# A transformer block's forward and backward on one core: the turn between the two passes rearranged

## The chip, the cores and the metric

The kernel runs on one core of a Trainium2 chip. The metric is device time in microseconds (us) of one execution; lower is better. Engines are named as in the profile: PE (TensorE, matrix products), PEld (its weight loads), DVE (VectorE), ACT (ScalarE), POOL (GpSimd), SP (SyncE). SP and POOL issue nearly all DMAs here, each from an in-order queue.

## The reference

One token (`x` of 640 values) goes through attention over a cache of 8192 keys with 32 heads of 192, and then through an MLP; both are wrapped in a conditioned layer norm. The outputs are the result and the gradients by `x`, the K and V caches, `wq`, `wo`, `w3`, `w4`, `c` and `w_mod`.

```python
mod = (silu(c) @ w_mod).reshape(1, 6, 1, -1)        # sa, ca, ga, sb, cb, gb
h = layernorm(x) * (1 + ca) + sa
q = h @ wq                                          # 32 heads of 192
p = softmax(q k^T * 192 ** -0.5); o = p v           # per head, 8192 keys
x = x + ga * (o @ wo)
h = layernorm(x) * (1 + cb) + sb
x = x + gb * B(h)
# B with S = 1: the shifted mixing term is zero, so
# B(h) = h + gelu(layernorm(h) @ w3) @ w4           # 640 -> 1536 -> 640
# outputs: x, and the vector-Jacobian product with grad_out for
# x, k_cache, v_cache, wq, wo, w3, w4, c, w_mod
```

K and V are 100.7 MB each, and so are dK and dV. K and V are read in the forward pass, V once more in the backward pass, and dK and dV are written there.

## The kernel before, in words

**Tiles.** Keys lie as 128 partitions by 64 (`J`). A head's K, V, dK or dV is two halves, each a tile of 128 x 32 x 192 in bf16 (1536 KB). K halves, and later dV and dK halves, rotate through five tiles of the pool `big`. V halves go through three tiles (`fv`), and in the backward pass through three more (`bv`), which are laid over the memory of the forward products (`fprod`) and of the scaled keys (`fek`).

**Forward loop** (`for i in range(1, HQ + 2)`). Head `i` gets its scores: DVE multiplies K with the broadcast q (`fwd_mult`, recorded under the helper's line L131, tile `prod`), PE sums over the 192 with an identity matrix (`fwd_ssum`, L355), DVE reduces (`fwd_red`, L359), PE and DVE find the maximum, ACT takes the exponential (`fwd_exp`, L376) with its row sum. Meanwhile head `i - 1` is worked off in four quarters: ACT and DVE scale K's rows by E into `EK` (`fwd_scale_act`, L390; `fwd_scale_dve`, L398), with E itself as a further column, and PE multiplies V with EK (`fwd_kvA`, L415; `fwd_kvB`, L423; `fwd_kvK`, L431). These products give o, and V^T E K, which is kept per head in `MA_all` and `MB_all`: with it the backward pass has dq without reading K again. `fwd_ao` (L475) adds each pair of heads' o @ wo to `ao_c`. The loop's last two passes only work off the last head (31).

**The turn.** W3 and W4 are loaded on POOL's queue into three `big` tiles in the last passes. `dg_some` (L496) takes products of W4 with the incoming gradient on DVE. `w3T_some` (L622) transposes W3 on PE, with ACT copies, in 15 groups of four blocks, some inside the gaps (`fill`) of the layer norms' short chains (`ln_cols`, `ln_bwd_cols`). Then come the two layer norms, W3's product u (L727), gelu and its derivative, dn2 by the transposed W3 (L755), the two layer norms' backward, and do of the last pair of heads by the transposed Wo (L1065). `ring_load` reads V halves and batches of Wo ahead on SP, in a ring of six slots.

**Backward loop** (`for i in range(HQ)`, heads 31 down to 0). DVE multiplies V with do in place (`bwd_mult`, tile `V_sb`), PE sums it (dP, L886). dV is the outer product of p and do, 20 rows of a half on ACT (L894) and 12 on DVE (L871), stored by POOL (L900). `bwd_ds` gives dS, and `bwd_dk` the outer product of dS and q, stored by POOL (L915). `hook` works off Wo's batches (`bwd_ttr`) and dq by `MA_all` and `MB_all` (`fin_dq_mm`, `fin_dq`). Further jobs for dWq, dWo, dW3, dW4 and dw_mod are hung into fixed passes.

The order on PE, DVE and ACT is the written one: `pin_order` ties each instruction to the one before it on its engine. DMA queues are in written order too, each DMA waiting for its tile.

Of the kernel before, what the change touches and what calls it, by code (L numbers as in the profile page):

```python
# [20 lines left out]
def kernel(  # L21
# [97 lines left out]
    nc.vector.memset(eps_c, LN_EPS)  # L119
    mask_lo = const.tile([P, 1], FP32, name="mask_lo")  # L120
# [31 lines left out]
    def ln_cols(x_c, pfx, fill=lambda k: None):  # L152
# [11 lines left out]
        nc.scalar.activation(out=std, in_=v_ps, func=ACT.Sqrt, bias=eps_c[:, 0:1], scale=1.0)  # L164
        rstd = ccol(1, pfx + "_rstd")
        nc.vector.reciprocal(out=rstd, in_=std)
        fill(1)
# [54 lines left out]
    big = ctx.enter_context(tc.tile_pool(name="big", bufs=5))  # L222

    def big_tile(name):
        return big.tile([P, JH, DH], BF16, name=name, tag="big")
# [61 lines left out]
    q_ps = kb_ps[:, 512 - NQC : 512]  # L287
# [32 lines left out]
    def load_v(pool, h, t):  # L320
        tl = pool.tile([P, JH, DH], BF16, name="V_sb")
        nc.sync.dma_start(out=tl, in_=V_hd[h][:, t * JH : (t + 1) * JH, :])
        return tl

    def load_fwd(h, t, kind):
        if not 0 <= h < HQ:
            return
        if kind == "v":
            st[h]["V"].append(load_v(fv, h, t))
        elif (h, t) not in K_st:  # L330
            K_st[h, t] = load_k(h, t)
# [40 lines left out]
    def fwd_exp(h, st):  # L372
        negm = fsm.tile([P, 1], FP32, name="negm")
        nc.vector.tensor_reduce(out=negm, in_=st["sm"][:, P : 2 * P], axis=AX.X, op=ALU.max, negate=True)  # L374
        E_f = fsm.tile([P, J], FP32, name="E_f")
        nc.scalar.activation(out=E_f, in_=st["sm"][:, 0:J], func=ACT.Exp, bias=negm, scale=1.0, accum_out=rowsum[:, h : h + 1])  # L376
        st["E_f"], st["EK"] = E_f, []

# [6 lines left out]
    def fwd_scale_act(h, q, st):  # L385
        t, r = divmod(q, 2)
        EK = fek.tile([P, JQ, DE], BF16, name="EK")
        for jj in range(NA):
            j = q * JQ + jj
            nc.scalar.activation(out=EK[:, jj, 0:DH], in_=K_st[h, t][:, r * JQ + jj, :], func=ACT.Copy, scale=st["E_f"][:, j : j + 1])  # L390
        st["EK"].append(EK)

# [15 lines left out]
    def fwd_kvA(h, q, st):  # L408
        (a0, a1), _, _, _, _ = head_split(h)
        if q == 0:  # L410
            st["A_ps"], st["B_ps"] = bank("a"), bank("b")
        t, r = divmod(q, 2)
        V_sb, EK = st["V"][t], st["EK"][q]
        for jj in range(JQ):
            nc.tensor.matmul(st["A_ps"][:, 0 : DH + 1], lhsT=V_sb[:, r * JQ + jj, a0:a1], rhs=EK[:, jj, 0 : DH + 1], start=(q == 0 and jj == 0), stop=(q == 3 and jj == JQ - 1))  # L415

    def fwd_kvB(h, q, st):
        _, (b0, b1), _, _, _ = head_split(h)
        t, r = divmod(q, 2)
        V_sb, EK = st["V"][t], st["EK"][q]  # L420
        for jj in range(JQ):
            g = 64 * (jj % 2)
            nc.tensor.matmul(st["B_ps"][g : g + 64, 0 : DH + 1], lhsT=V_sb[:, r * JQ + jj, b0:b1], rhs=EK[:, jj, 0 : DH + 1], start=(q == 0 and jj < 2), stop=(q == 3 and jj >= JQ - 2))  # L423

    def fwd_kvK(h, q, st, last=False):
        if h == HQ - 1 and not last:
            return
        EK = st["EK"][q]
        for jj in range(0, JQ, 2):
            g = 32 * (jj // 2 % 4)  # L430
            nc.tensor.matmul(kb_ps[g : g + 32, 0 : 2 * DH], lhsT=hot_bf[:, HQ - 1 - h : 2 * HQ - 1 - h], rhs=EK[:, jj : jj + 2, 0:DH], start=(h == 0 and q == 0 and jj < 8), stop=(h == HQ - 1 and q == 3 and jj >= JQ - 8), skip_group_check=True)  # L431
# [12 lines left out]
    def fwd_keep(h, st):  # L444
        (a0, a1), (b0, b1), bp, ca_, cb_ = head_split(h)
        op = 64 - bp
        nc.scalar.copy(out=MA_all[:, h, :], in_=st["A_ps"][:, 0 : DH + 1])
        Bt = fsm.tile([P, DH + 1], FP32, name="Bt")
        nc.scalar.copy(out=Bt[bp : bp + 64, :], in_=st["B_ps"][op : op + 64, 0 : DH + 1])
        st["Bt"] = Bt  # L450

    def fwd_keepB(h, st):
        (a0, a1), (b0, b1), bp, ca_, cb_ = head_split(h)
        Bt = st["Bt"]
        add(MB_all[bp : bp + 64, h // 2, :], st["B_ps"][bp : bp + 64, 0 : DH + 1], Bt[bp : bp + 64, :])
# [15 lines left out]
    def fwd_ao(hp, wo, sm):  # L471
        c0 = 3 * hp
        for r in range(NDC):
            for cc in range(3):
                nc.tensor.matmul(sm[:, 408 + r : 409 + r], lhsT=wo[:, cc, r * P : (r + 1) * P], rhs=o_col_bf[:, c0 + cc : c0 + cc + 1], start=(cc == 0), stop=(cc == 2))  # L475

    def fwd_ao_add(hp, sm):
        if hp == 0:
            dve_copy(ao_c, sm[:, 408 : 408 + NDC])
        else:  # L480
            add(ao_c, ao_c, sm[:, 408 : 408 + NDC])
# [4 lines left out]
    def w3n(i, lo, hi):  # L486
        return w_t[0][:, i * F + lo : i * F + hi] if i < 4 else w_t[1][:, lo:hi]

    def w4n(f, lo, hi):
        return w_t[1][:, F + f * D + lo : F + f * D + hi] if f < 7 else w_t[2][:, (f - 7) * D + lo : (f - 7) * D + hi]  # L490

    def dg_some(f0, f1):
        jk_t = fpr.tile([P, JH, DH], BF16, name="prod").rearrange("p j d -> p (j d)")
        for f in range(f0, f1):
            jk = jk_t[:, f % 4 * D : (f % 4 + 1) * D]
# [6 lines left out]
    warm = ccol(1, "warm")  # L502
# [18 lines left out]
    fv = ctx.enter_context(tc.tile_pool(name="fv", bufs=3, side="right", reuse_waits="tile"))  # L521
# [5 lines left out]
    fek_cm = tc.tile_pool(name="fek", bufs=4, reuse_waits="tile")  # L527
# [4 lines left out]
    for i in range(1, HQ + 2):  # L532
        if i == HQ + 1:
            nc.scalar.activation(out=warm, in_=eps_c, func=ACT.Sqrt)
# [4 lines left out]
        if pp:  # L539
            fwd_kv(i - 2, 3, st[i - 2])  # L540
# [7 lines left out]
        if i == HQ - 1:  # L548
            w_t = [flat(big_tile(f"w_t{k}")) for k in range(2)]
            nc.gpsimd.dma_start(out=w_t[0].rearrange("p (i n) -> p i n", n=F), in_=B_w3[0 : 4 * P, :].rearrange("(i p) n -> p i n", p=P))  # L550
            nc.gpsimd.dma_start(out=w_t[1][:, 0:F], in_=B_w3[4 * P : 5 * P, :])
            nc.gpsimd.dma_start(out=w_t[1][:, F : F + 7 * D].rearrange("p (f n) -> p f n", n=D), in_=B_w4[0 : 7 * P, :].rearrange("(f p) n -> p f n", p=P))
        if i == HQ:
            w_t.append(flat(big_tile("w_t2")))
            nc.gpsimd.dma_start(out=w_t[2][:, 0 : 5 * D].rearrange("p (f n) -> p f n", n=D), in_=B_w4[7 * P : 12 * P, :].rearrange("(f p) n -> p f n", p=P))
# [41 lines left out]
        load_fwd(i + 2, 0, "k")  # L597
        if n:
            fwd_mult(i + 1, 0, st[i + 1])
        if c:  # L600
            fwd_pairs(i, st[i])
        if i == HQ:
            dg_some(0, 7)
    dg_some(7, NFC)
    SB = [1024]
    w_t.append(flat(big_tile("w_t3")))
    NB3 = JH * DH // P

    def w3T(blk, n=1):
        if blk < NB3:  # L610
            return w_t[3][:, blk * P : (blk + n) * P]
# [3 lines left out]
    w3T_next = [0]  # L615

    def w3T_some(n):
        for g in range(w3T_next[0], min(w3T_next[0] + n, NFC * NDC // 4)):
            t_ps = bank("s", 2, "t_ps", SB[0])
            for k in range(4):  # L620
                f, i = divmod(4 * g + k, NDC)
                nc.tensor.matmul(t_ps[:, k * P : (k + 1) * P], lhsT=w3n(i, f * P, (f + 1) * P), rhs=ident_bf, start=True, stop=True)  # L622
            nc.scalar.copy(out=w3T(4 * g, 4), in_=t_ps[:, 0:512])
        w3T_next[0] += n

# [11 lines left out]
    w3T_some(3)  # L637
    fwd_kvK(HQ - 1, 0, st[HQ - 1], True)
    fwd_kvK(HQ - 1, 1, st[HQ - 1], True)
    sm = bank_c("sm_ps")  # L640
    fwd_ao(HH - 1, st[HQ - 1]["wo"], sm)
    fwd_ao_add(HH - 1, sm)
    fwd_kvK(HQ - 1, 2, st[HQ - 1], True)
    kb_sb = const.tile([P, 2 * DH], FP32, name="kb_sb")
# [3 lines left out]
    psum_cm.__exit__(None, None, None)  # L648
# [499 lines left out]
```

## Time and profile before

| | |
|---|---|
| median of 3 runs | 1395.56 us (1395.42 to 1396.38) |
| profiled execution | 1394.78 us, span 1393.0 us |
| PE busy | 864.9 us (62%) |
| DVE busy | 1072.7 us (77%) |
| ACT busy | 962.8 us (69%) |
| DMA moved | 570.81 MB, mean 410 GB/s; SP's queue 339.16 MB, POOL's 229.85 MB |
| mean granted PE clock | 0.78 |

The profile is of one execution; its own time is 0.78 us below the median. Busy shares are averages over stages with different limits: the forward pass is the first 550 us, the turn some 40 us, the backward pass the rest. Windows and timelines count from the span's start. "Idle before <-X" in a timeline is how long the engine had been idle ahead of an instruction, and what ended that.

### The profile page before, as it was taken

To read this page: it belongs to the slowest core of one execution; us is meant where nothing else is said; L and a number is where in the kernel's file an instruction comes from. 1 tells how busy PE (TensorE), PEld (TensorE's weight loads), DVE (VectorE), ACT (ScalarE), POOL (GpSimd) and SP (SyncE) were. 2 spreads that over 40 slices of the span, in tenths; PEclk is the share of its full clock that TensorE was granted. 3 is DMA by queue.
4 is the path that set the end of the run, shared out by engine and by line. 5 is a ranking of instruction groups with operands and counts; after the bars stand their busy time and mean duration, and the time that the engine had idled before them with its cause. 6 is when DMAs were issued, how large, how long until landed. Compare 5 with 4: busy or idle time off the path is not lost. (4 is left out here: it accounts for less than half of the span.)

```text
span 1393.0 us, 28144 instructions
## 1 busy us (share of the span) xinstructions
PE 864.9 (62%) x11519; PEld 676.1 (49%) x11519; DVE 1072.7 (77%) x1276; ACT 962.8 (69%) x2633; POOL 115.2 (8%) x207
## 2 busy tenths in 40 slices
PE   3799999999999999747636652444332444322442
PEld 3577777777777777535525541223221233212331
DVE  3588788887788877699978974975767659667796
ACT  1387778787788777686885586567666766556582
POOL 0000000000000000011101110211111111111011
PEclk9799999999999999566656666666776666765666
DMA  9999999999999999699999999999999999999988
GB/s 393 414 417 420 419 419 421 418 417 417 410 415 420 406 421 353 234 376 398 426 426 426 426 428 426 428 427 427 429 426 424 424 425 422 421 419 415 412 375 369
DMA packets 71711, 570.81 MB, mean 410 GB/s; under 512 B 6878, under 2 KB 18398, under 8 KB 31134
## 3 DMA queue, kind: packets, MB, share of 16 engines
q1 hardware_dynamic: 46496, 339.16, 59.2%
q0 software_dynamic: 25056, 229.85, 39.2%
q8 instruction: 90, 1.47, 0.4%
q14 instruction: 39, 0.32, 0.1%
q10 hardware_dynamic: 30, 0.00, 0.0%
HBM read 343.08 MB, written 225.91 MB: 408 GB/s over the span
## 5 line engine op out<-in xcount | busy, mean ns | idle before, releaser
L894 ACT ACTIVATE dV<-do_pb,PF 128x192 bf16<-128x192 bf16 x1260 | 439.5, 440 | 87.6 <-DMA out_dram<-dK 59.6
L886 PE MATMUL dP_ps<-V_sb,ident_bf 128*128 128x256 bf16 x1536 | 235.3, 329 | 256.1 <-DVE V_sb L131 256.0
L390 ACT ACTIVATE EK<-K_sb,E_f 128x192 bf16<-128x192 bf16 x1024 | 362.4, 442 | 4.0 <-PE kb_ps L294 2.6
L886 PEld LDWEIGHTS <-ident_bf 128*128 128x128 bf16 x1536 | 180.9, 118 | 310.9 <-issue 179.4
L871 DVE TENSOR_TENSOR dK<-dS,q_pb 128x6144 bf16<-128x6144 bf16 (+1 forms) x67 | 213.0, 3211 | 42.6 <-DMA out_dram<-dK 39.0
L131 DVE TENSOR_TENSOR prod<-K_sb,q_pb 128x6144 bf16<-128x6144 bf16 x64 | 214.3, 3349 | 5.4 <-DMA K_sb<-in_A_k_cache_dram 5.4
L131 DVE TENSOR_TENSOR V_sb<-V_sb,do_pb 128x6144 bf16<-128x6144 bf16 x64 | 211.8, 3351 | 6.9 <-DMA V_sb<-in_A_v_cache_dram 6.9
L415 PE MATMUL ps_a<-EK,V_sb 128*128 128x193 bf16 x2048 | 199.9, 250 | 2.8 <-DMA V_sb<-in_A_v_cache_dram 2.2
L415 PEld LDWEIGHTS <-V_sb 128*128 128x128 bf16 x2048 | 171.8, 99 | 21.5 <-issue 13.9
L871 DVE TENSOR_TENSOR dV<-P2h,do_pb 128x2304 bf16<-128x2304 bf16 (+1 forms) x65 | 87.3, 1369 | 57.6 <-DMA out_dram<-dV 50.4
L398 DVE TENSOR_TENSOR EK<-K_sb,P2h 128x1536 bf16<-128x1536 bf16 x128 | 121.3, 948 | 0.0
L423 PE MATMUL ps_b<-EK,V_sb 128*64 128x193 bf16 x2048 | 112.4, 252 | 0.0
L355 PE MATMUL S_ps<-prod,ident_bf 64*64 64x256 bf16 x3072 | 101.9, 281 | 13.4 <-DVE prod L131 13.4
L355 PEld LDWEIGHTS <-ident_bf 64*64 64x64 bf16 x3072 | 86.9, 111 | 33.5 <-issue 29.2
L423 PEld LDWEIGHTS <-V_sb 128*64 128x64 bf16 x2048 | 84.3, 110 | 20.2 <-issue 16.6
L376 ACT ACTIVATE E_f<-sm_ps,negm 128x64 f32<-128x64 f32 x32 | 10.1, 315 | 108.2 <-DVE negm L374 108.2
L359 DVE TENSOR_REDUCE S<-S_ps 128x128 f32<-128x1024 f32 x32 | 39.2, 1225 | 47.5 <-PE S_ps L355 47.5
L900 POOL DMA_DIRECT2D out_dram<-dV x65 | 34.9, 536 | 461.7 <-ACT dV L894 288.0
L431 PE MATMUL kb_ps<-EK,hot_bf 128*32 128x384 bf16 x1024 | 66.2, 337 | 0.0
L972 PEld LDWEIGHTS <-ident_bf 128*128 128x128 bf16 x112 | 13.9, 124 | 86.7 <-issue 83.1
L194 ACT CAST do_pb<-bc_ps 128x384 bf16<-128x384 f32 x16 | 7.5, 470 | 69.1 <-PE bc_ps L190 69.1
L930 ACT ACTIVATE wq_o<-wq_bc,ha_f 128x1536 bf16<-128x1536 bf16 x12 | 18.5, 1566 | 47.6 <-DMA out_dram<-wq_o 47.6
(249 smaller groups left out, 820.0 us busy)
## 6 DMA issues: line engine op xcount, KB each, us to landing
V_sb<-in_A_v_cache_dram SPq DMA_DIRECT2D x126, 1536.0 KB, 13.7
K_sb<-in_A_k_cache_dram SPq DMA_DIRECT2D x64, 1536.0 KB, 14.4
out_dram<-dV POOLq DMA_DIRECT2D x63, 1536.0 KB, 19.4
out_dram<-dK POOLq DMA_DIRECT2D x63, 1536.0 KB, 20.6
wq<-in_A_wq_dram SPq DMA_DIRECT2D x3, 2560.0 KB, 34.0
wo_t<-in_A_wo_dram SPq DMA_DIRECT2D x16, 480.0 KB, 14.4
out_dram<-dwo POOLq DMA_DIRECT2D x16, 480.0 KB, 19.5
wq<-in_A_wq_dram SPq DMA_DIRECT2D x4, 1920.0 KB, 29.4
```

The costliest lines, as they stand in the source:

```text
L131: nc.vector.tensor_tensor(out=out, in0=a, in1=b, op=ALU.mult)
L355: nc.tensor.matmul(st["S_ps"][c0 : c0 + 64, r, t * JH : (t + 1) * JH, :], lhsT=ident_bf[64 * r : 64 * r + 64, 64 * r : 64 * r + 64], rhs=p ...
L359: nc.vector.reduce_sum(out=st["S2"], in_=st["S_ps"], axis=AX.X)
L390: nc.scalar.activation(out=EK[:, jj, 0:DH], in_=K_st[h, t][:, r * JQ + jj, :], func=ACT.Copy, scale=st["E_f"][:, j : j + 1])
L398: nc.vector.tensor_tensor(out=EK[:, NA:JQ, 0:DH].rearrange("p j (d r) -> p j d r", r=2), in0=K_st[h, t][:, r * JQ + NA : (r + 1) * JQ, :]. ...
L415: nc.tensor.matmul(st["A_ps"][:, 0 : DH + 1], lhsT=V_sb[:, r * JQ + jj, a0:a1], rhs=EK[:, jj, 0 : DH + 1], start=(q == 0 and jj == 0), sto ...
L423: nc.tensor.matmul(st["B_ps"][g : g + 64, 0 : DH + 1], lhsT=V_sb[:, r * JQ + jj, b0:b1], rhs=EK[:, jj, 0 : DH + 1], start=(q == 0 and jj < ...
L431: nc.tensor.matmul(kb_ps[g : g + 32, 0 : 2 * DH], lhsT=hot_bf[:, HQ - 1 - h : 2 * HQ - 1 - h], rhs=EK[:, jj : jj + 2, 0:DH], start=(h == 0 ...
L871: nc.vector.tensor_tensor(out=o.rearrange("p j (d r) -> p j d r", r=2), in0=pairs[:, :, None, :].to_broadcast([P, n, NP2, 2]), in1=vec.rea ...
L886: nc.tensor.matmul(bst[h]["dP_ps"][:, t * JH : (t + 1) * JH, :], lhsT=ident_bf, rhs=V_sb[:, :, k * DS : (k + 1) * DS], start=(k == 0), sto ...
L894: nc.scalar.activation(out=o[:, jj, :], in_=doh, func=ACT.Copy, scale=bst[h]["PF"][:, j0 + jj : j0 + jj + 1])
L900: st2.dma_start(out=dV_hd[h][:, j0 + r0 : j0 + r1, :], in_=o[:, r0:r1, :])
```

## The change

The last head (31) gets no scaled keys and no products V^T E K. Its o comes from 128 products with single columns of E (`sum_rows`, `fwd_o_mm`), its exponentials are written in bf16 straight into `E_all`, and its dq comes in the backward pass from its unscaled K, which stays in two `big` tiles until then (`dq_last`). The forward loop ends one head earlier. W3 and W4 are loaded on SP's queue, behind K and V of the last heads. The second V half of head 30 stays in its tile and isn't read again. `fprod`'s and `fek`'s memory becomes free earlier, so that V halves are read ahead sooner; the first Wo batch goes into a `big` tile instead of a ring slot. The transposes of W3, the d_g products and h2 are cut in pieces and put in other gaps. u, dn2, h2, do and the last dq use spare columns of the PSUM bank of `kb_ps`. Head 31's dV is made by DVE alone, its first half stored in three pieces; the first dV half of head 30 is moved ahead of the loop. The order of the `big` tiles is written out by hand.

```diff
...
-        E_f = fsm.tile([P, J], FP32, name="E_f")
+        E_f = E_all[:, h, :] if h == HQ - 1 else fsm.tile([P, J], FP32, name="E_f")
...
+    def sum_rows(ps, c0, tl, cols, h, first, last):
+        (a0, a1), (b0, b1), bp, _, _ = head_split(h)
+        rows = tl.rearrange("p j d -> p (j d)")
+        for r in range(JH):
+            nc.tensor.matmul(ps[:, c0 : c0 + 1], lhsT=tl[:, r, a0:a1], rhs=cols[r], start=(first and r == 0), stop=(last and r == JH - 1), skip_group_check=True)
+        for r in range(JH):
+            lo, p0 = (r * DH + b0, bp) if r == 0 else (r * DH + b0 - bp, 0)
+            nc.tensor.matmul(ps[p0:P, c0 + 1 : c0 + 2], lhsT=rows[:, lo : r * DH + b1], rhs=cols[r], start=False, stop=(last and r == JH - 1), skip_group_check=True)
+
+    def fwd_o_mm(h, t, st):
+        if t == 0:
+            st["o_ps"] = st["sm"][:, 416:418]
+        sum_rows(st["o_ps"], 0, st["V"][t], [E_all[:, h, j : j + 1] for j in range(t * JH, (t + 1) * JH)], h, t == 0, t == 1)
...
+    def load_w(k):
+        w_t.append(flat(big_tile(f"w_t{k}")))
+        if k == 0:
+            nc.sync.dma_start(out=w_t[0][:, F : F + 7 * D]..., in_=B_w4[0 : 7 * P, :]...)
+        elif k == 1:
+            nc.sync.dma_start(out=w_t[1]..., in_=B_w3[0 : 4 * P, :]...)
+            nc.sync.dma_start(out=w_t[0][:, 0:F], in_=B_w3[4 * P : 5 * P, :])
+        else:
+            nc.sync.dma_start(out=w_t[2][:, 0 : 5 * D]..., in_=B_w4[7 * P : 12 * P, :]...)
...
-    for i in range(1, HQ + 2):
+    for i in range(1, HQ):
...
         load_fwd(i + 2, 0, "k")
+        if i == HQ - 2:
+            load_w(0)
+        if i == HQ - 1:
+            fwd_wo(i, st[i])
+            load_w(1)
+            load_w(2)
...
+    dg_some(2)
+    fwd_kvA(hl - 1, 3, st[hl - 1])
+    fwd_kvB(hl - 1, 3, st[hl - 1])
+    fwd_keep(hl - 1, st[hl - 1])
+    nc.scalar.activation(out=warm, in_=eps_c, func=ACT.Sqrt)
+    fwd_keepB(hl - 1, st[hl - 1])
+    fwd_tot(hl, sl_["sm"])
+    fwd_o_mm(hl, 0, sl_)
+    dg_some(2)
+    fwd_rinv(hl, sl_["sm"])
+    fwd_o_prev(hl - 1)
+    fwd_o_mm(hl, 1, sl_)
+    dg_some(1)
+    fwd_o_last(hl, sl_)
+    fwd_ao(HH - 2, st[hl - 2]["wo"], sl_["sm"])
+    fwd_kvK(hl - 1, 3, st[hl - 1])
+    nc.scalar.copy(out=kb_sb, in_=kb_ps[:, 0 : 2 * DH])
+    fwd_ao_add(HH - 2, sl_["sm"])
...
-    w3T_some(3)
-    fwd_kvK(HQ - 1, 0, st[HQ - 1], True)
-    fwd_kvK(HQ - 1, 1, st[HQ - 1], True)
-    sm = bank_c("sm_ps")
-    fwd_ao(HH - 1, st[HQ - 1]["wo"], sm)
-    fwd_ao_add(HH - 1, sm)
+    fwd_ao(HH - 1, sl_["wo"], sl_["sm"], 420)
+    dg_some(1)
+    fwd_ao_add(HH - 1, sl_["sm"], 420)
...
-    V_b = {HS[0]: st[HS[0]]["V"]}
+    V_b = {HS[0]: st[HS[0]]["V"], HS[1]: {1: st[HS[1]]["V"][1]}}
...
+    big_order[:] = [0, 4, 1, 4, 1, 2, 3, 4, 1, 2, 3, 4, 0, 1] + [2, 3, 4, 0, 1] * HQ
...
+    def ln1_fill(k):
+        if k == 0:
+            dg_some(1)
+        else:
+            w3T_pe(4)
+            w3T_act(4)
+
+    def ln2_fill(k):
+        w3T_pe(1 + 2 * k)
+        dg_some(1)
...
-    n1_c, r1 = ln_cols(x1_c, "ln1", lambda k: w3T_some(k + 1))
-    fwd_kvK(HQ - 1, 3, st[HQ - 1], True)
+    n1_c, r1 = ln_cols(x1_c, "ln1", ln1_fill)
...
-    w3T_some(2)
...
+    dg_some(2)
+    w3T_act(4)
+    w3T_pe(6)
...
-    w3T_some(15)
+    w3T_act(1)
+    w3T_pe(1)
+    w3T_act(6)
+    load_wo(0, big_tile("V_sb"))
...
-    for i in range(NDC):
-        for f in range(NFC):
+    for f in range(NFC):
+        for i in range(NDC):
...
+    def lb2_fill():
+        woT_some(2)
+        h2_mm()
...
     def lb1_fill():
-        woT_some(1)
-        q_pb[PS[0]] = pair_bc(bsm, q_bf, PS[0], "q_pb")
-        nc.scalar.copy(out=kb_sb, in_=kb_ps[:, 0 : 2 * DH])
+        woT_some(2)
+        q_pb[PS[0]] = pair_bc(bsm, q_bf, PS[0], "q_pb", bank("s", 2, "t_ps", SB[0]))
...
+    def dq_last(h):
+        for t in range(2):
+            sum_rows(dql_ps, 0, K_st[h, t], [bst[h]["dS2"][:, j, 0:1] for j in range(t * JH, (t + 1) * JH)], h, False, t == 1)
...
-    bwd_dv(HS[0], 0, 0, 2)
-    c_first = fin_c(PS[0], 1)
-    bwd_dv(HS[0], 1)
+    o0 = tw.tile([P, JH, DH], BF16, name="dV", tag="w3T_t")
+    bwd_dv_dve(o0, HS[0], 0, 0, (8, 16, JH))
+    bwd_dv_dve(big_tile("dV"), HS[0], 1, 0, (JQ, JH))
+    bwd_pf(HS[1])
+    o1 = big_tile("dV")
+    bwd_dv_act(o1, HS[1], 0, 0, JQ)
+    bwd_dv_store(o1, HS[1], 0, 0, JQ)
+    bwd_dv_act(o1, HS[1], 0, JQ, 26)
+    pairs_outer(o1[:, 26:JH, :], bst[HS[1]]["P2h"][:, 26:JH, :], vec_of(do_pb, HS[1]), JH - 26)
+    bwd_dv_store(o1, HS[1], 0, JQ, JH)
...
-                bwd_mult(h, t)
+                bwd_mult(h, t, 2 if i == 0 else 1)
+                if i == t == 0:
+                    ring_load()
+                    c_first = fin_c(PS[0], 1)
...
         bwd_ds(h)
+        if i == 0:
+            dq_last(h)
...
```

`w3T_pe(n)` and `w3T_act(n)` are the two halves of `w3T_some`, transposes and copies, now over six PSUM buffers; `load_wo(k, tile)` reads a batch of Wo into a tile; `fwd_o_prev` and `fwd_o_last` divide the o of heads 30 and 31 by their row sums; `bwd_dv_dve` makes rows of dV on DVE and stores them in pieces, `bwd_dv_act` makes rows on ACT.

## The prediction

> **What bounds the kernel now.** I read the page first. Its slices show the DMA engines full nearly everywhere, and one hole, in slices 16 and 17, the turn from the forward pass to the backward pass.
>
> ```profile
> DMA  9999999999999999699999999999999999999988
> GB/s 393 414 417 420 419 419 421 418 417 417 410 415 420 406 421 353 234 376 398 426 426 426 426 428 426 428 427 427 429 426 424 424 425 422 421 419 415 412 375 369
> ```
>
> DMA sets the time: 570.81 MB at some 425 GB/s are 1343 us of the span of 1393.0. The rest is mostly idle DMA, at the start, at the end and in the turn. What an edit is worth is therefore the idle DMA time that it removes. Next, the windows over the turn (start:end, length, then busy us of PE, PEld, DVE, ACT, POOL, then the granted clock, the DMA share and GB/s):
>
> ```profile
> 540.00:550.00 10.00, 9.30 (x138) 7.47 (x137) 4.53 (x13) 7.31 (x23) 0.00 (x0) 0.99 0.96 369
> 550.00:560.00 10.00, 9.06 (x143) 6.92 (x140) 9.22 (x29) 8.56 (x21) 0.00 (x0) 1.00 0.73 263
> 560.00:570.00 10.00, 7.08 (x94) 5.60 (x95) 4.59 (x24) 4.71 (x9) 0.00 (x0) 0.53 0.75 261
> 570.00:580.00 10.00, 8.52 (x126) 7.29 (x124) 4.47 (x30) 6.79 (x16) 0.00 (x0) 0.50 0.52 217
> 580.00:590.00 10.00, 5.99 (x99) 5.52 (x97) 8.46 (x9) 9.14 (x27) 1.60 (x3) 0.50 0.40 158
> 590.00:600.00 10.00, 7.81 (x51) 5.89 (x51) 9.83 (x18) 10.00 (x30) 0.57 (x2) 0.76 0.78 277
> 600.00:610.00 10.00, 0.79 (x8) 0.51 (x8) 9.93 (x6) 4.51 (x14) 1.60 (x3) 0.58 0.98 393
> ```
>
> Against 425 GB/s these seven windows lack 10.4 MB, or 24 us. The reads of the turn dry up at 575; DMA then stands still until the first gradient store, and is full again from about 605. So the clock that matters is the first dV store. The timeline gives the chain to it: the last head's product waits for K, then its softmax, LN1's mean, and at last dV.
>
> ```profile
> 533.16 3.36 DVE L131 TENSOR_TENSOR prod<-K_sb,q_pb 128x6144 bf16<-128x6144 bf16 x1 [2.05 <-DMA K_sb<-in_A_k_cache_dram]
> ...
> 542.63 0.31 ACT L376 ACTIVATE E_f<-sm_ps,negm 128x64 f32<-128x64 f32 x1 [5.70 <-DVE negm L374]
> ...
> 548.44 0.53 PE L475 MATMUL sm_ps<-o_col_bf,wo_t 128*128 128x1 bf16 x15
> ...
> 568.57 1.74 PE L727 MATMUL ps_a<-n_bf,w_t 128*128 128x1 bf16 x60
> ...
> 581.64 3.43 DVE L871 TENSOR_TENSOR dV<-P2h,do_pb 128x3072 bf16<-128x3072 bf16 x2 [1.11 <-ACT do_pb L194]
> ```
>
> POOL's timeline shows the stores themselves; it had waited 43.84 us for the first.
>
> ```profile
> 583.70 0.56 POOL L900 DMA_DIRECT2D out_dram<-dV  x1 [43.84 <-DVE dV L871]
> 585.36 0.56 POOL L900 DMA_DIRECT2D out_dram<-dV  x1 [1.11 <-DVE pc L131]
> 589.51 0.53 POOL L900 DMA_DIRECT2D out_dram<-dV  x1 [3.59 <-ACT PF L702]
> ```
>
> When the first store starts, both versions have read the same tiles (all weights, V of heads 30 and 29, the first Wo batch). The bytes left are equal, so the shift of this store is the gain, plus or minus what the first backward heads lose.
>
> **Part by part.** *Weights behind V.* The second K half of head 31 was issued at 514.92 and landed 18.2 us later (median of K loads 14.4); the W3 load of 1536 KB, issued on POOL at 520.7, ran beside it. Now 1120 KB of W4 go in that place on SP's queue, behind K and V, and the rest behind head 31's V. SP comes to them in its order: the first after K of head 29 is scaled (520), the next when K of head 30 is (531, 538), and head 31's V never waits for one of these. The product loses its 2.05 wait; PE, which idled 1.73 and dropped its clock, lets the reduction run behind the two EK pieces, at 536.4 instead of 539.22. I take **-2.8** for the softmax of head 31 (bounds 0 and -3.5).
>
> *Head 31 without key-value products.* From its exp (542.63) to LN1's mean (PE, 562.75) lie 20.1 us: ACT scales K (11.3), PE does 160 products, ACT and DVE copy, and the last addition to ao queues behind five d_g reductions of 0.75. After: head 30's three remaining groups (3.1 less the 0.4 already running at exp), the row totals (0.4), 128 one-column products of V with E, handovers between PE and DVE in one PSUM tile (0.6), o and its cast (0.7), two Wo groups and head 30's last kb group (1.6), one d_g and the additions (1.2). No row shows one-column products with V as weights. The nearest are the Wo ones, 15 in 0.53, and W3's, 60 in 1.74: 29 to 35 ns. The far bound is a weight load beside wide matmuls (page: 99 to 118 ns), 14 us in all. I take 35, so 4.5. The sum is 11.7: **-8.4** (bounds -9.2 and +1.1).
>
> *The MLP's own chain.* LN1's mean to the first store: 20.95 us, at the clock of 0.50. Each W3 group of four transposes costs PE 0.5 and ACT 0.55 (0.59 alone). Three groups that ran before LN1 now come after it. Four groups in LN1's gap in place of two and a kb group put LN2's mean back by 0.6; four in LN2 delay u by another 0.6; at the end of W3 the order by f lets dn2 follow the copies and stands at +1.1 in all. In lb2's gap two Wo groups and the 60 products of h2 (1.8) stand ahead of lb1's mean: +1.4. In lb1's gap a second Wo group, and q's broadcast, which waits for a PSUM buffer, hold do back: +0.8. The d_g pieces (0.82) fit in DVE's waits. The first store now follows 8 rows (0.87) in place of 16 (1.72): -0.85. Sum **+2.5** (bounds 0 and +5, as no trace shows this order).
>
> First store: 583.7 - 2.8 - 8.4 + 2.5 = 575.0, a shift of **-8.7**.
>
> *One V read less, Wo and V earlier.* 1.57 MB would be 3.7 us of full DMA, but reads end before the first store in either version. The Wo batch needs W3's tile, free only after the last transpose (some 563), and lands by 569. All hidden: 0; if the store came sooner than I think, the reads' end would be the next limit.
>
> *After the first store.* For: dV of head 30 starts on ACT at once, its first tile ready some 5 us sooner against the first store. Against: DVE now makes both dV tiles of head 31 alone (6.9 where it had 4.8), PE does 96 narrower products for 48, and the V reads that follow are freed about 2 us later against the store. DVE is busy 98% from 590 to 610, so it cannot run ahead of this. Net 0 (bounds -3 and +4). The 128 products for head 31's dq (4.5 on PE) follow dS; queued behind them on PE are the broadcast for pair 14 and head 30's dP, whose V product DVE reaches only after 6.6 us of dK: 0. The second dK tile takes the first K buffer, whose 64 products (2.2) end inside the first dK tile (3.3). SP's queue holds nothing that is due sooner. A few copies and memsets of 0.17 in dq come where DMA, not DVE, is the limit: 0.
>
> The profiled execution took 1394.78 (span 1393.0), 0.78 under the median 1395.56. Minus 8.7 that is 1386.1, or 1386.9 on the median: **1387**. This measurement can tell some 0.2%, 2.8 us, from no change.
>
> **Rivals.** *Full clock in the turn.* PE is 85% busy in 570 to 580 at a granted clock of 0.50, mostly with one-column matmuls, and I keep that clock. If the removed pause before LN1 (3.0 us) kept it at 1.00, a transpose group would cost 0.31 (8 in 0.62 at 556.5) in place of 0.5; the 19 groups (15 of W3, 4 of Wo) would take 3.7 us less, of which I count 3 on the chain: 1384. For: the clock was 1.00 until that pause. Against: near-full business did not bring it back. The Trainium skill (TensorE: Matmul & The Clock Gate, Part 1: The HAM clock gate) says that the half clock follows an idle stretch and that about 3.4 us of sustained activity end it; by that rule the time would be 1384, while this trace, with 20 us at 0.50 and PE 72% busy, disagrees.
>
> *Weights late.* W3 now lands behind head 31's V, by conservation of the bytes at about 546, W4's rest at 548. Should it be 555, the transposes in LN1's gap hold PE, and u behind them: +3.5, 1390.4.
>
> *Write buffers, the slow side.* The five large tiles held dV and dK as soon as K was used. Now K of head 31 keeps two until its dq is done, and the Wo batch keeps one until the third head: four or fewer serve the stores for three heads. A tile takes 7.0 to fill (20 ACT rows) and a median of 19.4 to land; four tiles per head through four buffers make 26.4 per head, where DMA needs 22.1 (9.44 MB). Three heads lose 13 us: 1400. It decides as soon as landing stays near 19 us with fewer stores queued. Against: landing is mostly queueing. The first two half-tiles landed in 5.3, and the trace's waits for these buffers are spread over the run while DMA stays full. At half price it leaves 1393.5, no change.
>
> *The change not doing what it says.* If K of head 31 lands no sooner, only the 2.8 is gone: 1389.7, inside the forecast's range.
>
> **Chances.** Forecast 0.57 (its own range 1382 to 1391), full clock 0.15, weights late 0.10, half-price buffers 0.08, full-price buffers or dear V products 0.10. Below 1392.8: 0.82; within 0.2%: 0.08; slower: 0.10. The range takes in full clock with a good start of the backward pass, 1380, and the half-price buffers, 1395.
>
> **What would show it.** Head 31's exp near 539.8 with no DMA wait before its product; LN1's mean near 551.5; the first dV store near 575; 125 V loads; clock 0.50 from LN1 to do; over 350 GB/s in the 20 us after the first store has got going, and no wait of DVE on dV or dK stores in the first three heads. Wrong if the chain from LN1 to the store is much over 21 us, if the 128 products take over 6 us, or if DMA falls below 400 GB/s again between 600 and 660, other than where Wo rows are read.

## The result, and the profile after

Four runs of the changed kernel have a median of 1382.51 us (1381.09 to 1384.36); four of the kernel before, on the same chip, 1395.49 (1394.17 to 1396.38). The ratio is 0.9909, with a 95% interval of 0.9891 to 0.9926: 13.0 us less. Run again later, it was 0.9926 (0.9912 to 0.994), 10.3 us less. The forecast was 1387.0. The profiled execution took 1381.49 us, with a span of 1379.7.

The slices of the page after: the hole in slices 16 and 17 is still there, but shallower. Its 234 GB/s have become 305, and 353 before it 388.

```profile
GB/s 392 415 415 419 419 417 420 418 419 418 406 420 419 404 419 388 305 378 422 416 425 427 426 426 428 426 424 420 408 428 425 412 426 427 429 425 412 414 399 366
```

The windows over the turn, with the columns of the prediction (PE, PEld, DVE, ACT, POOL, granted clock, DMA share, GB/s):

```profile
540.00:550.00 10.00, 8.37 (x202) 7.14 (x202) 6.30 (x25) 2.60 (x5) 0.00 (x0) 0.82 1.02 392
550.00:560.00 10.00, 9.17 (x124) 8.87 (x125) 7.55 (x35) 7.46 (x16) 0.00 (x0) 0.50 1.01 416
560.00:570.00 10.00, 8.05 (x174) 7.47 (x171) 4.00 (x24) 6.12 (x15) 0.00 (x0) 0.67 0.61 211
570.00:580.00 10.00, 3.46 (x29) 3.36 (x29) 9.97 (x9) 9.17 (x27) 3.88 (x7) 0.50 0.78 310
580.00:590.00 10.00, 7.31 (x92) 7.09 (x90) 9.72 (x23) 7.02 (x20) 0.53 (x1) 0.80 0.91 343
590.00:600.00 10.00, 4.74 (x135) 4.35 (x135) 10.00 (x5) 5.14 (x15) 1.07 (x2) 0.54 1.00 384
600.00:610.00 10.00, 7.55 (x48) 5.60 (x47) 9.90 (x15) 10.00 (x30) 0.53 (x1) 0.78 0.95 335
```

The seven windows now move 23.9 MB where they moved 19.4: against 425 GB/s they lack 5.8 MB, or 13.7 us, where they lacked 24.4. DMA now stays full until 560, where it had fallen off at 550, and the stores start at 570: the window between them, with 211 GB/s, is most of what is left of the hole. DMA's share is back at 0.78 in the next, but at 310 GB/s, and at 343 in the one after that.

The timeline of the changed kernel gives the chain to the first store: head 31's product, its exp, the 128 products of V with E (L480 and L483), the means of LN1, LN2, lb2 and lb1 (all L150), do's product, dV, and the store on POOL.

```profile
531.36 3.35 DVE L132 TENSOR_TENSOR prod<-K_sb,q_pb 128x6144 bf16<-128x6144 bf16 x1
...
539.55 0.31 ACT L380 ACTIVATE E_all<-sm_ps,negm 128x64 bf16<-128x64 f32 x1 [2.29 <-DVE negm L378]
...
542.41 0.94 PE L480 MATMUL sm_ps<-E_all,V_sb 128*128 128x1 bf16 x32
543.28 1.05 PE L483 MATMUL sm_ps<-E_all,V_sb 128*64 128x1 bf16 x32
544.60 0.94 PE L480 MATMUL sm_ps<-E_all,V_sb 128*128 128x1 bf16 x32 [0.26 <-DVE rinv_bc L466]
545.47 1.15 PE L483 MATMUL sm_ps<-E_all,V_sb 128*64 128x1 bf16 x32
549.78 0.56 PE L150 MATMUL ln_m<-ln_s,negd_mat 128*128 128x1 f32 x2 [0.94 <-DVE ln_s L155]
552.97 0.54 PE L150 MATMUL ln_m<-ln_s,negd_mat 128*128 128x1 f32 x2
...
562.94 0.38 PE L150 MATMUL lb_m<-lb_s,negd_mat 128*128 128x2 f32 x2 [0.53 <-DVE lb_s L177]
565.35 0.57 PE L150 MATMUL lb_m<-lb_s,negd_mat 128*128 128x2 f32 x2
567.31 0.59 PE L1172 MATMUL kb_ps<-dao_bf,wo_t 128*128 128x1 bf16 x15
569.21 5.16 DVE L967 TENSOR_TENSOR dV<-P2h,do_pb 128x1536 bf16<-128x1536 bf16 x4 [1.11 <-ACT do_pb L195]
570.48 0.68 POOL L992 DMA_DIRECT2D out_dram<-dV  x1 [568.83 <-DVE dV L967]
```

The product has no DMA wait in front of it any more. ACT's exp stands at 539.55 (542.63 before), LN1's mean at 549.78 (562.75), the first store at 570.48 (583.70). The kernel before has its own rows for the means and for do's product:

```profile
562.75 0.56 PE L149 MATMUL ln_m<-ln_s,negd_mat 128*128 128x1 f32 x2 [3.05 <-DVE ln_s L154]
...
576.12 0.59 PE L149 MATMUL lb_m<-lb_s,negd_mat 128*128 128x2 f32 x2
...
578.09 0.59 PE L149 MATMUL lb_m<-lb_s,negd_mat 128*128 128x2 f32 x2 [0.51 <-DVE lb_s L176]
...
579.79 0.54 PE L1065 MATMUL do_ps<-dao_bf,wo_t 128*128 128x1 bf16 x15 [0.45 <-DVE dao_bf L131]
```

From these rows, the same stretches in both kernels:

| stretch | before | after | change | forecast |
|---|---|---|---|---|
| to head 31's exp | 542.63 | 539.55 | -3.1 | -2.8 |
| exp to LN1's mean | 20.12 | 10.23 | -9.9 | -8.4 |
| LN1's mean to lb2's mean | 13.37 | 13.16 | -0.2 | +1.1 |
| lb2's mean to lb1's mean | 1.97 | 2.41 | +0.4 | +1.4 |
| lb1's mean to do's product | 1.70 | 1.96 | +0.3 | +0.8 |
| do's product to the first store | 3.91 | 3.17 | -0.7 | -0.85 |
| first store | 583.70 | 570.48 | -13.2 | -8.7 |
| span | 1393.0 | 1379.7 | -13.3 | -8.7 |

### The profile page after: what moved, and what is told of

Same layout as the page of the kernel before. It is cut to its first block, busy times and chain, and to the rows that moved or that the text cites. A ratio compares the mean times of both kernels' runs of the same rounds, so it can differ in the third digit from the quotient of the medians.

```text
span 1379.7 us, 28361 instructions
## 1 busy us (share of the span) xinstructions
PE 854.9 (62%) x11655; PEld 675.5 (49%) x11655; DVE 1071.3 (78%) x1275; ACT 945.1 (69%) x2585; POOL 113.5 (8%) x206
## 5 line engine op out<-in xcount | busy, mean ns | idle before, releaser
L989 ACT ACTIVATE dV<-do_pb,PF 128x192 bf16<-128x192 bf16 x1246 | 434.5, 439 | 115.3 <-DMA out_dram<-dK 61.1
L984 PE MATMUL dP_ps<-V_sb,ident_bf 128*128 128x256 bf16 (+1 forms) x1584 | 231.4, 322 | 259.0 <-DVE V_sb L132 259.0
L394 ACT ACTIVATE EK<-K_sb,E_f 128x192 bf16<-128x192 bf16 x992 | 351.1, 442 | 4.0 <-PE kb_ps L298 2.7
L984 PEld LDWEIGHTS <-ident_bf 128*128 128x128 bf16 x1584 | 181.2, 117 | 309.4 <-issue 174.4
L132 DVE TENSOR_TENSOR V_sb<-V_sb,do_pb 128x6144 bf16<-128x6144 bf16 (+1 forms) x66 | 212.0, 3253 | 0.0
L419 PE MATMUL ps_a<-EK,V_sb 128*128 128x193 bf16 x1984 | 194.2, 250 | 1.6 <-DMA V_sb<-in_A_v_cache_dram 1.5
L419 PEld LDWEIGHTS <-V_sb 128*128 128x128 bf16 x1984 | 166.8, 99 | 19.4 <-issue 12.7
L967 DVE TENSOR_TENSOR dV<-P2h,do_pb 128x2304 bf16<-128x2304 bf16 (+2 forms) x67 | 89.1, 1353 | 54.9 <-DMA out_dram<-dV 49.6
L1021 POOL DMA_DIRECT2D out_dram<-dK x67 | 36.9, 551 | 145.8 <-DVE dK L967 103.5
L191 PE MATMUL bc_ps<-ident_bf,dq_bf 128*128 128x128 bf16 x48 | 6.4, 304 | 63.8 <-ACT do_pb L195 62.4
## 6 DMA issues: line engine op xcount, KB each, us to landing
out_dram<-dV POOLq DMA_DIRECT2D x61, 1536.0 KB, 21.9
```

Of the source, the lines that this page charges most:

```text
L132: nc.vector.tensor_tensor(out=out, in0=a, in1=b, op=ALU.mult)
L394: nc.scalar.activation(out=st["EK"][q][:, jj, 0:DH], in_=K_st[h, t][:, r * JQ + jj, :], func=ACT.Copy, scale=st["E_f"][:, j : j + 1])
L419: nc.tensor.matmul(st["A_ps"][:, 0:n], lhsT=V_sb[:, r * JQ + jj, a0:a1], rhs=EK[:, jj, 0:n], start=(q == 0 and jj == 0), stop=(q == 3 and ...
L967: nc.vector.tensor_tensor(out=o.rearrange("p j (d r) -> p j d r", r=2), in0=pairs[:, :, None, :].to_broadcast([P, n, NP2, 2]), in1=vec.rea ...
L984: nc.tensor.matmul(bst[h]["dP_ps"][:, t * JH + r : t * JH + r + n, :], lhsT=ident_bf, rhs=V_sb[:, :, k * DS : (k + 1) * DS], start=(k == 0 ...
L989: nc.scalar.activation(out=o[:, jj, :], in_=vec_of(do_pb, h), func=ACT.Copy, scale=bst[h]["PF"][:, t * JH + jj : t * JH + jj + 1])
```

## Experiments

The theory was that the shift of the first dV store is the gain, since everything ahead of it is one chain and everything behind it is DMA. Its rivals were: the saved or earlier reads bring the time, not the chain; the PE clock does; the tiles that hold dV and dK until they are stored take some of it back. The kernels were run in three groups, each with runs of the kernel before in it; every ratio below is to those of its own group.

**The change once more.** 

> The changed kernel as it is, beside the three variants of it in this comparison. All theories: some 13 us under the kernel before, a ratio near 0.991, first dV store 13 us earlier than before's 583.7. It sets how far single executions of it scatter; its profiled ones so far span 1379.3 to 1382.6.

Measured: 1385.34 us (1384.72 to 1386.0), first store at 571.13. It gained 10.3 us for a shift of 12.6, where the first run of the same code gained 13.0 for 13.2. The chains of the two differ by 0.65 us, their spans by 3.9 (1383.6 and 1379.7); the rest arises behind the first store, and where isn't settled (from 620 to 1340 DMA runs at 421 and 422 GB/s, which over 720 us is some 2 us). Differences of some 2 us between two kernels say little here, even less between groups.

**The chain made longer.** DVE does more work of a kind that is in the program anyway, into memory that nobody reads (`d_g` gets the same values again), just ahead of LN1:

```diff
+    for k in range(13):
+        f = k % 7
+        j0 = 5 * D + 12 * P + f % 2 * D
+        nc.vector.tensor_tensor_reduce(out=w_t[2][:, j0 : j0 + D], in0=w4n(f, 0, D), in1=dbo_bc, ..., accum_out=d_g[:, f : f + 1])
     x1_c = ccol(NDC, "x1_c")
```

> Changed kernel with 13 further d_g reductions on DVE (0.745 each, 9.7 us) between ao and LN1, results unchanged. Theory (the shift of the first dV store is the gain): first store 9.7 later, near 580.2, and the time 9.7 longer than the changed kernel's, about 1392. Rival (the gain comes from fewer and earlier reads, the chain is only along for the ride): reads still end at the same time, so less than 3 us longer.

Measured: 1394.22 us, ratio 0.9999 (0.9981 to 1.0017). The timeline of this kernel has LN1's mean 10.63 us after PE's last work, and the first store at 581.43:

```profile
560.42 0.56 PE L150 MATMUL ln_m<-ln_s,negd_mat 128*128 128x1 f32 x2 [10.63 <-DVE ln_s L155]
...
581.43 0.68 POOL L996 DMA_DIRECT2D out_dram<-dV  x1 [579.78 <-DVE dV L971]
```

The store is 10.3 us later than in the unchanged run beside it, and the time 8.9 us longer: with the tiles and all reads as the change has them, except that the first Wo batch follows the chain (issued at 571.06, in the change at 560.44), a late chain takes the gain away but for 1.4 us by the medians. The rival of the reads falls.

**The saved read put back.** Head 30's second V half is read again:

```diff
-    ... HS[1]: {1: st[HS[1]]["V"][1]}}
+    ... HS[1]: {}}
...
     ring_load()
+    V_b[HS[1]][1] = load_v(fv, HS[1], 1, 1)
```

> Changed kernel that reads the second V half of head 30 again (1.57 MB, 3.7 us of full DMA) behind the three prefetched V halves, as the kernel before did. Theory: reads still end before the first store (V of head 29 some 3.7 later, Wo's batch near 569), so within 1 us of the changed kernel. Rival (bytes count wherever they stand): 3.7 us longer.

Measured: 1383.77 us, ratio 0.9916 (0.9903 to 0.993), first store 571.44. The window from 560 to 570 of this kernel has DMA full where the change has its hole (211 GB/s):

```profile
560.00:570.00 10.00, 8.42 (x178) 7.84 (x176) 4.24 (x28) 6.34 (x14) 0.00 (x0) 0.67 0.96 375
```

The 1.57 MB went into that hole and cost nothing that can be told from scatter. "One V read less: 0" was right, though a DMA-bound kernel with less to move seems to ask for more: the byte that is saved was not moved at a time when DMA was the limit.

**The store alone made later.** The stores of head 31's two dV halves are written behind the making of both, the second half's first:

```diff
-    bwd_dv_dve(o0, HS[0], 0, 0, (8, 16, JH))
-    bwd_dv_dve(big_tile("dV"), HS[0], 1, 0, (JQ, JH))
+    o0b = big_tile("dV")
+    for t, o, ends in ((0, o0, (0, 8, 16, JH)), (1, o0b, (0, JQ, JH))):
+        for ra_, rb_ in zip(ends, ends[1:]):
+            pairs_outer(...)
+    bwd_dv_store(o0b, HS[0], 1, 0, JH)
+    bwd_dv_store(o0, HS[0], 0, 0, JH)
```

> Changed kernel with the same pieces of head 31's dV on DVE, but both halves stored only when both are made: first store 5.6 later (576.1 for 570.5), DVE's work at the same times. Theory (DMA's start sets the time): DMA loses 5.6 us before the store and gets some 2.4 back where the changed kernel's DMA ran dry behind the first stores, so 3 us longer (2 to 5.6). Rival (the first heads are bound by DVE, busy 98%, so do's arrival counts and not the store): no difference.

Measured: 1382.85 us, ratio 0.9908 (0.9895 to 0.9922). The edit didn't do what it was meant to. The first half's store left at 572.95, as soon as that half was made and ahead of the second half's (576.29), although the edit writes it last: POOL's stores don't always go in the written order. The first store is thus only 1.8 us behind the unchanged run beside it, 2.5 behind the change's first profile, and the time is not longer; that is within the scatter.

In a second attempt one row of each half is made last, so that no half can leave before both are done. 

> Changed kernel with one row of each half of head 31's dV made last, so that neither half can be stored before all of it is made (the other delayed-store kernel moved its first store by only 2.5). DVE's work is as long as before by 0.2. First store of head 31 near 576.2 for 570.5. Theory (the first store's time is the gain): 3 to 5.6 us longer than the changed kernel, ratio 0.994 to 0.996. Rival (do's arrival counts: DVE starts its 98% busy stretch then, and DMA makes up a late start of the stores out of the queue): within 1.5 us of the changed kernel, ratio 0.991 to 0.993.

Measured: 1390.0 us, ratio 0.997 (0.9959 to 0.9981), with the first store, one of head 30, at 575.33 and head 31's two at 576.25. That is 4.7 us longer than the change took in its second run, and the gain over the kernel before is 4.4 us where it was 10.3: 5.8 less, just above what the theory said, with a ratio outside both forecasts. But the waits of this kernel show something of its own (engine, tile, line, what it waited for; us in all, times, longest):

```profile
ACT dao_bc L195 <- DMA out_dram<-dV: 10.3, 1, 10.3
...
DVE c_bc L198 <- PE c_ps L145: 5.7, 1, 5.7
```

`dao_bc` lies over head 31's first dV tile, so that ACT waited 10.3 us until that store had landed, and DVE 5.7 behind it. Whether it is the store's time as such that counts, or the arrival of do, from which all engines go on, stays open: the extra wait spoils this test, and in all other kernels but the one just above both move together. There do came as early as in the change, the store 2.5 us later, and the time did not grow; that speaks for do, but 2.5 us is little more than the scatter.

**Weights on POOL's queue.** The MLP's weights go back to the queue they had, and all else of the change stays:

```diff
     def load_w(k):
...
-            nc.sync.dma_start(out=w_t[0][:, F : F + 7 * D]...)
+            nc.gpsimd.dma_start(out=w_t[0][:, F : F + 7 * D]...)
...
```

> Changed kernel with W3 and W4 loaded on POOL's queue again, at the same places of the program. Theory: the loads compete with K of head 31, whose second half lands some 4 us later as before; the product waits about 2 us, head 31's exp comes near 542.5 instead of 539.6, the first dV store 3 us later, and the time is 2 to 4 us longer than the changed kernel's. Rival (all loads share one DMA capacity, the queue does not matter): exp within 0.5 of 539.6 and no difference in time.

Measured: 1388.61 us, ratio 0.9955 (0.9943 to 0.9968); the kernel with 64 streamed columns (below), which has the weights on SP and is of the same group, took 4.3 us less. The timeline of this kernel:

```profile
533.76 3.36 DVE L132 TENSOR_TENSOR prod<-K_sb,q_pb 128x6144 bf16<-128x6144 bf16 x1 [2.14 <-DMA K_sb<-in_A_k_cache_dram]
...
541.99 0.31 ACT L380 ACTIVATE E_all<-sm_ps,negm 128x64 bf16<-128x64 f32 x1 [4.55 <-DVE negm L378]
...
551.99 1.01 PE L480 MATMUL sm_ps<-E_all,V_sb 128*128 128x1 bf16 x32 [5.20 <-DMA V_sb<-in_A_v_cache_dram]
```

The first wait is the one that the prediction costed: 2.14 us, and exp 2.4 us later than in the change. The second is new, and larger: without the key-value products, o wants head 31's second V half at 544.60 (change) where it was wanted at 551.71 (before), and the weights of the other queue run beside that half too. PE stood for 5.20 us. LN1's mean moved to 557.22, the first store to 578.25. That is 7.5 us behind the kernel with 64 columns (570.75), of which only the 4.3 us show in the time.

**One part alone, on the kernel before.** First the weights on SP's queue, at the place in the program where POOL had them:

```diff
         if i == HQ - 1:
             w_t = ...
-            nc.gpsimd.dma_start(...)
+            nc.sync.dma_start(...)
```

> Kernel before with one part of the change: its W3 and W4 loads issued on SP's queue at the place where they stand, everything else as before. Theory: K of head 31 lands without company, exp near 539.7 for 542.63, the first store near 580.8 for 583.7, the time 3 us shorter, ratio 0.998. Rival: no difference.

Measured: 1393.58 us, ratio 0.9986 (0.9977 to 0.9995): 1.2 us. The exp came at 539.64, as early as in the change, but the gain was gone later. The weights now stood ahead of head 31's second V half on SP, and the timeline shows PE waiting for it; LN1's mean is at 561.10 and the first store at 582.06.

```profile
550.40 1.53 PE L415 MATMUL ps_a<-EK,V_sb 128*128 128x193 bf16 x16 [1.62 <-DMA V_sb<-in_A_v_cache_dram]
```

Then three quarters of head 31's scaled keys and key-value products dropped:

```diff
     def fwd_scale(h, q, st):
+        if h == HQ - 1 and q > 0:
+            st["EK"].append(st["EK"][0])
+            return
...
+        if h == HQ - 1 and q > 0:        # in fwd_kvA, fwd_kvB and fwd_kvK
+            return
```

> Kernel before with three of the four quarters of head 31's key scaling and of its V products left out (ACT 8.4 us, DVE 3.5, PE 96 products; the kb products of those quarters use the first quarter's scaled keys; o, ao and dq of that head are those of a quarter of its keys). Theory: the turn's chain from exp to LN1 is shortened by some 8 us, so is the first store (near 575.5), and the time is 7 to 9 us shorter, ratio near 0.994. Rival (the turn is bound by its reads): reads end as before near 575, so at most 2 us shorter.

Measured: 1394.43 us, ratio 0.9996 (0.9988 to 1.0005). 8 us of store shift were expected and 2.3 came. The timeline says what stepped in:

```profile
549.33 0.83 DVE L505 CUSTOM_DVE_ANT_0 prod<-w_t,dbo_bc 128x640 bf16<-128x640 bf16 x1 [0.72 <-DMA w_t<-in_B_w_dram]
...
555.81 0.54 PE L484 MATMUL sm_ps<-o_col_bf,wo_t 128*128 128x1 bf16 x15 [5.34 <-DVE o_col_bf L197]
...
560.40 0.56 PE L149 MATMUL ln_m<-ln_s,negd_mat 128*128 128x1 f32 x2 [3.29 <-DVE ln_s L154]
```

Seven d_g reductions of 0.82 stand on DVE ahead of o, and wait for W4 until 549.33; PE waits 5.34 us for o. Five more stand ahead of the last addition to ao: 3.29. The key-value products had covered them.

Last, the same with the d_g reductions moved into the gaps of LN1, LN2, u and gelu. 

> Kernel before with three quarters of head 31's key scaling and V products left out as in the kernel of that kind above (o, ao and dq of that head are those of a quarter of its keys), and with the twelve d_g reductions moved from ahead of ao into the gaps of LN1, LN2, u and gelu. Theory: without that, d_g on DVE (8.9 us) had taken the place of the products (first store only 2.3 earlier); now LN1's mean comes near 551 for 560.4, some 4.8 of d_g still stand on the MLP's chain, the first store near 576 (7 earlier than before's 583.7), the time 5 to 7 us shorter than before, ratio 0.995 to 0.9965. Rival (the turn waits for its reads): ratio above 0.998.

Measured: 1391.46 us, ratio 0.9975 (0.9966 to 0.9985), first store 578.72. LN1's mean came at 553.97 where 551 was said. The reductions are off the chain to LN1, and PE waits next for a batch of Wo:

```profile
552.47 0.56 PE L484 MATMUL sm_ps<-o_col_bf,wo_t 128*128 128x1 bf16 x15 [1.80 <-DMA wo_t<-in_A_wo_dram]
```

That batch had been issued at 534.85, with the weights on POOL's queue beside it; that they held it up is likely but no run separates it. Behind LN1 the reductions are on the chain: from LN1's mean to the first store it takes 24.8 us where it took 20.95, and PE waits 3.24 for du.

So none of the parts does much alone: weights 1.2 us, products 0.4, products with d_g 3.0, and all of the change 10 to 13. Each time that one cause of delay was taken away, another was ready a little behind it.

**The clock.** The 128 products of the changed kernel stream 64 equal columns in place of one, and a further place in PSUM is used for them:

```diff
-            nc.tensor.matmul(ps[:, c0 : c0 + 1], lhsT=tl[:, r, a0:a1], rhs=cols[r], ...)
+            nc.tensor.matmul(ps[:, c0 : c0 + 64], lhsT=tl[:, r, a0:a1], rhs=cols[r].to_broadcast([P, 64]), ...)
```

> Changed kernel whose 128 products for head 31's o stream 64 equal columns instead of one (results unchanged), to ask what the granted clock follows. If it follows the columns streamed, the clock stays at 1.00 from 542 to 550 (now 0.82), the matmuls of LN1's mean take 0.38 instead of 0.56, and the MLP's chain to the first store is 1 to 2 us shorter. If it follows PE's busy time or nothing that these products change: the same clock, the products some 4.2 us as now or up to 2.5 us longer at half clock, and the time the same or up to 2.5 longer.

Measured: 1384.31 us, ratio 0.9921 (0.9906 to 0.9936), first store 570.75: no gain. But the clock did what was asked. The window of this kernel, and the means of LN1 and LN2 in its timeline:

```profile
540.00:550.00 10.00, 8.83 (x208) 7.56 (x202) 6.04 (x23) 2.84 (x7) 0.00 (x0) 1.00 1.01 390
```

```profile
550.45 0.39 PE L150 MATMUL ln_m<-ln_s,negd_mat 128*128 128x1 f32 x2 [0.94 <-DVE ln_s L155]
553.55 0.54 PE L150 MATMUL ln_m<-ln_s,negd_mat 128*128 128x1 f32 x2
```

The granted clock is 1.00 where the change had 0.82, LN1's mean in 0.39 in place of 0.56; LN2's mean, 3 us later, is back at 0.54. The wider products cost 1.15 and 1.28 per 32 (0.94 and 1.05), 0.8 us in all, more than the short full clock gave back: from the end of these products to LN1's mean it takes 2.8 us in place of 3.2. The clock did fall all the same, at 550.6. In the change it falls at 546.5, in the change run again at 545.1, so the moment varies from run to run, but in both it lies where one-column products were all that PE had.

**Write buffers.** dV and dK go through four large tiles for all heads, where the change has five after the turn:

```diff
-    big_order[:] = [0, 4, 1, 4, 1, 2, 3, 4, 1, 2, 3, 4, 0, 1] + [2, 3, 4, 0, 1] * HQ
+    big_order[:] = [0, 4, 1, 4, 1, 2, 3, 4, 1, 2, 3, 4] + [1, 2, 3, 4] * 2 * HQ
```

> Changed kernel that never again uses the Wo batch's large tile, so that dV and dK go through four large tiles in all 31 heads instead of five from the third head on. Rival of the prediction (a buffer is taken for 7.0 of filling and 19.4 of landing, so four make 26.4 us per head for 22.1): over 100 us longer, and in the changed kernel three heads would have lost 13. Theory (landing is queueing and shrinks with the queue; DMA stays full): less than 10 us longer over the 29 heads, under 1 us for three heads, and the median landing of dV falls below 17.

Measured: 1387.26 us, ratio 0.9942 (0.9928 to 0.9956): 2 to 5 us more than the changed kernel had, for some 29 further heads with four tiles. The DMA issues (count, KB each, median us from issue to landing), first of this kernel, then of the change:

```profile
out_dram<-dV POOLq DMA_DIRECT2D x61, 1536.0 KB, 15.6
```

```profile
out_dram<-dV POOLq DMA_DIRECT2D x61, 1536.0 KB, 21.9
```

With fewer tiles each store lands sooner: the landing time is mostly the wait behind other stores. Three heads with four tiles, as in the change, would by this cost a tenth of that, a few tenths of a microsecond.

**A tighter turn.** All of Wo's transposes go into lb2's gap, and h2 and q's broadcast behind do:

```diff
     def lb2_fill():
-        woT_some(2)
-        h2_mm()
+        woT_some(4)
     def lb1_fill():
-        woT_some(2)
-        q_pb[PS[0]] = pair_bc(...)
+        pass
```

> Changed kernel with the MLP's backward chain tightened: all four Wo transposes in lb2's gap, nothing in lb1's, h2's 60 products and q's broadcast behind do's broadcast. Theory: lb1's mean 0.2 earlier, do 0.4 to 0.8 earlier, the first store near 569.8 for 570.5 to 571.4; time 0.5 to 1 us shorter, ratio 0.990 to 0.992, at the limit of what can be told. Rival: the products moved behind do hold back the first heads' PE work, no difference or up to 1.5 longer.

Measured: 1385.19 us (1383.11 to 1396.1), ratio 0.9941 (0.9922 to 0.9961). From LN1's mean to the first store it takes 19.8 us in place of 20.7 (20.3 in the change run again), and the time shows nothing of it. One execution of this kernel, the profiled one, took 1396.1 us although its first store left at 570.77: from 620 to 1340 its DMA moved 415 GB/s in place of 422, which over 720 us is 12 us. What the turn gains can be lost again in the backward pass; why in this execution isn't known.

## Why the prediction came out as it did

The reading behind it held in the main: the kernel gains by idle DMA in the turn, and the first dV store, or do just ahead of it, is its clock. Over twelve measurements that differ from the kernel before in the turn (the change twice, and all others but the four-tile one; the profiled store against 583.70, the median against the kernel before in the same group), a line through zero gives 0.9 us of time for each us of the store's shift. Why not quite 1 wasn't settled. At the two ends, a shift of 12.3 to 13.2 gave 9.3 to 13.0 us, one of 1.6 to 2.3 gave 0.4 to 1.4. Between them single kernels lie further off: 8.4 gave 4.4 (with the extra wait on `dao_bc`), 10.8 gave 12.8.

The forecast shift of the store, -8.7, was too small: -13.2 and -12.6 were measured. That the second run's gain of 10.3 us still lies near the forecast is partly luck, since 2.3 us of its larger shift were lost behind the store. The terms, one by one:

*Weights behind V, -2.8.* Measured -3.1 to the exp, and 2.4 of it comes back when the weights go back to POOL. The step was right but too small in scope: in the changed kernel o needs head 31's V sooner, and there the same edit keeps another 5.20 us wait away. Its worth in place is 4.3 us.

*Head 31 without key-value products, -8.4.* Measured -9.9. The 128 products end some 4.2 us after they start, where 4.5 was taken (35 ns each; per 32 the rows are 0.94 to 1.15, 29 to 36 ns), so the nearest row was the right one and the far bound of 14 us was far off. That stretch already holds the handover in its middle, a wait of 0.26, which the sum had at 0.6 on top. Most of the other 1.2 us is that, and o's cast and the last additions, each 0.3 shorter than taken. Not seen was how much of this term belongs to other edits: with the products dropped alone, d_g on DVE holds o back, and with d_g spread, Wo is late. The term was right for the whole change only.

*The MLP's own chain, +2.5.* This is the term that failed, with -0.25 measured. LN2's mean follows LN1's by 3.19 us (3.17 before): the two further transpose groups in the gap, costed at +0.6, run while DVE and ACT do their steps, and most of what was put at +0.6 ahead of u does too (0.26 measured). W3's last transposes no longer hold up dn2, whose products follow u's by 4.5 us (555.88 to 560.33) where it was 5.0 (568.57 to 573.56). In all, from LN1's mean to lb2's, the chain is 0.2 shorter in place of 1.1 longer. The fillings of the lb2 and lb1 gaps cost 0.4 and 0.3 where 1.4 and 0.8 were taken. Up to lb2's mean the mistake is one: PE's and ACT's time for a filling was added to the chain, though most of it fits in the gap for which it was written. In lb2's gap the filling does overhang, since DVE was ready 0.7 us ahead of lb1's mean; there it was priced too high. The clock was 1.00 from 561 to 563 and helped: lb2's mean took 0.38 in place of 0.59, eight of Wo's transposes 0.73 in place of 1.01, and together with the overlap of these rows that is some 0.5 of the 1.0 us that this gap was off. In lb1's gap q's broadcast did hold do back, as said, but by 0.3.

*Reads, and what follows the first store, 0 each.* The V read: shown above. In the first profile the span fell by 13.3 for a store 13.2 earlier, so nothing was lost on balance; in the second it fell by 9.4 for 12.6. The term of 0 holds within its bounds of -3 and +4, not better. There is no wait of DVE on stores in the windows that were named; ACT waits once for 4.1 us on a dV store (4.9 before).

*The rivals.* Full clock in the turn: the window 550 to 560 has PE busy 92% at 0.50, and 560 to 570 has 0.67, so apart from the half microsecond in lb2's gap it isn't what brought the time under the forecast. In the change the clock fell at 546.5 although PE had been busy 94% of the time with the 128 one-column products, from 542.4 to 546.6; with 64 streamed columns it stayed at 1.00. The Trainium skill (TensorE: Matmul & The Clock Gate, Part 1: The HAM clock gate) has the half clock follow an idle stretch and about 3.4 us of sustained activity end it; by busy time this trace disagrees. By columns that flow through the array it agrees at this place, the only one that was tested. The prediction's count against it was off at one point: from 570 to 580 PE's busy time was not mostly one-column products, but 5.2 of 8.5 us of transposes, with pauses. Weights late: they were, by some 5 us for W4's rest (552.96 for 548), and it cost a wait of 0.16 on DVE. The transposes wait for ACT, not for DMA. Write buffers: rejected by the four-tile kernel; the premise that landing stays near 19 us was what failed. K no sooner: no, exp came at 539.55.

Of the signs that were named, exp, V loads (125), no waits of DVE on stores, and the 128 products under 6 us came as said; LN1's mean (549.78 for 551.5) and the first store (570.48 for 575) came earlier. The clock was not 0.50 all the way from LN1 to do, since it stood at 1.00 from 561 to 563. The DMA rate after the first store did not come as said: 310 GB/s from 570 to 580 and 343 from 580 to 590, where over 350 was said. From 600 to 610 it fell to 335. Wo's rows are read there from 607.58, but the fall began at 605, so this sign of being wrong appeared in part.

## What to carry to other kernels

Where a DMA-bound kernel has one hole, find the instruction that ends it and sum only the chain to that instruction; bytes saved inside the hole were worth nothing here. Before an edit is priced by the work that it removes, ask who arrives next: here four causes lay within a few microseconds of each other, and each edit alone gave 0 to 3 us of the 13. Work put in a gap of another engine's chain is to be priced by what overhangs the gap, not by its length; what does overhang, as in lb2's gap, at the clock that is then granted.

## What the runs showed of the hardware

Where it was tested, the granted clock went with what streams through PE, not with how long PE is busy: it fell from 1.00 to 0.50 at 546.5 with PE busy 94% with 128 one-column products, and the same products with 64 columns, in a window 88% busy, kept 1.00. What counts in general no run here shows. One-column products with new weights of 128 columns each took much the same at both clocks: 32 in 0.94 us at 1.00 (29 ns each), 60 in 1.78 at 0.50 (30 ns; the row at 555.88).

A second queue's load delayed what another queue had already issued: W3 and W4 on POOL held back a K half of SP by 2.1 us and a V half by 5.2, and the same bytes on SP's own queue, behind V, left no wait at either place.

A store's time from issue to landing, 15.6 us with four tiles and 21.9 with five, went with how many stores can be queued. By an estimate, 1536 KB at the 425 GB/s of the slices would take 3.7 us, and two stores of 384 KB at the start of the backward pass landed in 2.9.
